# A list scheduler's table of durations is replaced, and the row copies at a block's end go to other tiles

## The chip, the cores and the metric

The kernel runs on one core of a Trainium2 chip. The metric is the device time of one execution in microseconds, as the median of several runs. A core has a matrix engine (PE), a vector engine (DVE), a scalar engine (ACT), a general engine (POOL), and a queue that only issues transfers (SP). Each works through its own list of instructions in a fixed order, and an instruction that waits holds back all that stand behind it on its engine.

## The reference

Attention over pooled keys and values, then two MLPs over 4608 tokens of width 512, all in float32:

```python
k_p, v_p = mean of k, v over groups of 8 positions     # 576 -> 72 per head
attn = softmax(q @ k_p.T / 8) @ v_p                    # 8 batches, 8 heads of 64
x = attn, heads side by side                           # 4608 x 512
h = x @ w_in                                           # 512 -> 2048
g = where(h >= 1, h, where(h <= -1, 0, (h + 1)**2 / 4))
y = g @ w_out                                          # 2048 -> 512
out = (sigmoid(y @ w_gate) * (y @ w_val)) @ w_out2     # 512 -> 1536 -> 512
```

## The kernel before, in words

A float32 product is made of three products of a cheaper format (`three`, L607 to L611): each operand is split into a high part, a cast, and a low part, the difference. The cast is made by ACT (L534), the difference by DVE (L543).

The tokens are cut into nine blocks of 512, the 2048 columns of `w_in` into sixteen steps of 128. Seven blocks go through the first MLP in the plain way described here, and the last two go through it later, by a scheme with seven products instead of eight, which is used for the second MLP too. In the first MLP step s (block s div 16, weight s mod 16) consists of two pieces of PE work:

- the **h step** s: four column products of three matmuls each, `h <- x, win` at L609 to L611, into one of two PSUM banks called h. The third matmul of a product, L611, is the first to read the low part of the weight `win`.
- the **y step** s: four products, `acc <- g, wj` at L609 to L611, which add to four accumulators called acc. For the first twelve steps it is four plain float32 products instead (L772, called plain products below, two matmul instructions each in the profile).

Between them ACT makes relu and square (L741, L743) and DVE the rest of g (L746), whose end also frees the h bank for h step s+2. ACT and DVE then split g, and split `wout_f` into `wj` (both L534 and L543).

While block 0 is worked on, the weights are fetched and prepared (`weight`, L556 to L600): abs and scaling on ACT (L580, L582), four bit operations on DVE (L585, L587, L590, L594), then cast and difference. Attention of later blocks goes on beside all of this, and after step 22 the weights of the second MLP are prepared and written to DRAM.

At the end of a block `out_rows` (L621) copies the four accumulators to SBUF, two to a tile, on ACT or DVE, and SP writes each tile to DRAM (`y`). For blocks 0 to 5 the first tile is `st`, with one buffer of its own, and the second is one of the two buffers of `raw`, which weight preparation also uses.

The order of instructions on each engine isn't written out. Each operation is entered by `op(engine, cost, key, fn, ...)` with a duration in microseconds. `Plan.issue` then plays a list scheduler: it keeps a modelled time for each engine, and of the operations that could start within 0.05 us of the earliest it issues the one with the smallest key. The durations decide nothing on the chip but this order, and which of two engines gets a copy that either could do. A result is taken to be usable 0.14 us after its duration ends. Transfers have their own model, which the change leaves alone.

Of the kernel before, what the change touches and what calls it, by code (L numbers as in the profile page):

```python
# [18 lines left out]
P = 128  # L19
POOL = 8  # L20
TB = 512
# [186 lines left out]
def pooled_attention_two_mlps(  # L208
# [77 lines left out]
    AC = {n: ac for n in ("kp", "q", "qT", "mx", "sm", "aq", "aT", "st")}  # L286
# [98 lines left out]
    def unit(j, p, T):  # L385
# [54 lines left out]
        for h in range(2):  # L440
# [106 lines left out]
    def reload(d, t, key, behind):  # L547
# [4 lines left out]
        op(ACT, 0.62, key - 2, lambda: nc.scalar.copy(out=t.t[:, 0], in_=vals()), r=[t], w=[t])  # L552
        op(DVE, 0.69, key - 1, lambda: nc.vector.tensor_tensor(
            out=t.t[:, 1], in0=vals(), in1=t.t[:, 0].bitcast(F32), op=ALU.subtract), r=[t], w=[t])

    def weight(w, m, cols, r, key, t=None, keep=None, spill=None):  # L556
# [37 lines left out]
        op(DVE, 0.7, key - 4, lambda: nc.vector.tensor_tensor(  # L594
# [18 lines left out]
    def columns(key, o, w, xs):  # L613
        last = []
        for c in range(KD):
# [3 lines left out]
            last = [op(PE, 0.65, key + 0.1 * c, mm, r=[w, xs[c]], w=[o], behind=last)]  # L619

    def out_rows(key, dst, accs, d=(), early=False):  # L621
        for i in range(2):
            st = buf_a("st", 1, [P, 2, TB]) if early and i == 0 else Buf(raw_p, "raw", 2, [P, 2, TB], fifo=None if early else True)
            for n, a in enumerate(accs[2 * i:2 * i + 2]):
                op((ACT, DVE), (0.48, 0.6), key, (
                    lambda st=st, a=a, n=n: nc.scalar.copy(out=st.t[:, n], in_=a.t),
                    lambda st=st, a=a, n=n: nc.vector.tensor_copy(out=st.t[:, n], in_=a.t)), r=[a], w=[st])
            op(SP, 0.475, key + 1, lambda st=st, i=i: nc.sync.dma_start(
                out=dst[2 * i * P:2 * (i + 1) * P, :].rearrange("(c p) t -> p c t", p=P), in_=st.t),
                r=[st], w=d, nbytes=P * DM * 8)  # L630


    zeros = memsets()
    xs_of = {}
# [65 lines left out]
    for j in range(NB1):  # L700
        if j >= XD:
            xs_of[j] = [buf_x() for _ in range(KD)]
            for c in range(KD):
                x, d = xs_of[j][c], x_d[j, c]
                T = due1(j * M1) - 12 + c
                op(SP, 0.475, T - 16, lambda x=x, d=d: nc.sync.dma_start(out=x.t[:, 1].bitcast(F32), in_=d.t), r=[d], w=[x], nbytes=P * TB * 4)
                high_part(T, x, Src(x, lambda t: t[:, 1].bitcast(F32)))
                op(DVE, 0.69, T + 1, lambda x=x: nc.vector.tensor_tensor(
                    out=x.t[:, 1], in0=x.t[:, 1].bitcast(F32), in1=x.t[:, 0].bitcast(F32), op=ALU.subtract), r=[x], w=[x])
        xs = xs_of.pop(j)  # L710
        for m in range(M1):
# [29 lines left out]
            op(ACT, 0.69, Tg, lambda t=t, hps=hps: nc.scalar.activation(  # L741
                out=t.t, in_=hps.t, func=AF.Relu, bias=half.t, scale=0.5), r=[hps, half], w=[t])
            op(ACT, 0.63, Tg + 1, lambda t=t: nc.scalar.activation(  # L743
                out=t.t, in_=t.t, func=AF.Square), r=[t], w=[t])
            o = g if plain else t
            op(DVE, 0.69, Tg + 2, lambda t=t, hps=hps, o=o: nc.vector.scalar_tensor_tensor(  # L746
# [22 lines left out]
            for c in range(KD):  # L769
# [143 lines left out]
    def out_part(gs, f, m, key, accs, last):  # L913
        g = buf_g()
        op2(ACT, 0.62, key - 5, lambda: nc.scalar.copy(out=g.t[:, 0], in_=gs.t[:, f]), r=[gs], w=[g])
        op2(DVE, 0.69, key - 4, lambda: nc.vector.tensor_tensor(
            out=g.t[:, 1], in0=gs.t[:, f], in1=g.t[:, 0].bitcast(F32), op=ALU.subtract), r=[gs, g], w=[g])
        w = w2[m]
        for c in range(4):
# [3 lines left out]
            last[c] = [op(PE, 0.65, key + 0.1 * c, mm, r=[w, g], w=[accs[c]], behind=last[c])]  # L923
# [10 lines left out]
    for i in range(MP):  # L934
# [4 lines left out]
        for n in range(2):  # L939
            sl, a21 = slots[n]  # L940
            for f in range(2):
                last = []
                for c in range(KD):
# [5 lines left out]
                    last = [op(PE, 0.65, T + 5.2 * n + 2.6 * f + 0.1 * c, mm, r=[sl, a21, xs[c]], w=[banks[n, f]], behind=last)]  # L949
# [3 lines left out]
        for f in range(2):  # L953
# [4 lines left out]
            op2(DVE, 0.69, T + 2.6 * f + 6, lambda t=t, f=f, gs=gs, pv=banks[1, f]: nc.vector.tensor_tensor(  # L958
# [45 lines left out]
    def out_pair(pr, hs, K0, KP):  # L1004
# [4 lines left out]
        def comb(key, h, n, x, y, alu, other=None):  # L1009
            op2(DVE, 0.69, key, lambda: nc.vector.tensor_tensor(out=h.t[:, n], in0=x(), in1=y(), op=alu),  # L1010
# [6 lines left out]
        def product(n, mat, o, start, what):  # L1017
            chain = []
            for i in range(MP):
# [14 lines left out]
                chain[:] = [op2(PE, 1.3, key, mm, r=[w, g] + ([] if start or i else o), w=o, behind=chain)]  # L1034
# [3 lines left out]
        def add(key, o, b, u):  # L1038
            for e in range(2):
                op2(DVE, 0.69, key, lambda e=e: nc.vector.tensor_tensor(  # L1040
# [47 lines left out]
        def to_bank(key, src, dst):  # L1088
            for e in range(2):
                op2(ACT, 0.6, key, lambda e=e: nc.scalar.copy(out=dst[e].t, in_=src.t[:, e]), r=[src], w=[dst[e]])  # L1090
# [300 lines left out]
```

## Time and profile before

| what | value |
|---|---|
| median of 3 runs | 1692.19 us (1691.58 to 1692.28) |
| the profiled execution | 1693.15 us |
| its span | 1691.4 us |
| PE busy | 1667.2 us, 99% |
| DVE, ACT, POOL busy | 69%, 57%, 14% |
| mean granted TensorE clock | 0.996 |

The span runs from the first to the last instruction of the program; what lies around it in the profiled execution is 1.75 us. Busy time of PE counts a matmul from its start to its modelled end, and matmuls overlap, so PE's idle time is what can be read from it, not its rate.

### The profile page before, as it was taken

How to read it: one execution, taken by the hardware profiler on the slowest of the kernel's cores; microseconds unless marked ns; L12 is line 12 of the kernel's file. 1: busy time of each engine (PE TensorE's matmuls, PEld its weight loads, DVE VectorE, ACT ScalarE, POOL GpSimd, SP SyncE). 2: the span in 40 equal slices, each digit the busy share in tenths (PEclk: the TensorE clock that was granted, in tenths of full speed). 3: DMA queues.
4: the chain of work that ended last, by engine and by line, in shares of the span. 5: the costliest groups of instructions: out<-in, count | busy, mean ns of one | idle time of the engine just before them, and what ended most of it. 6: DMA issues, size and time to landing. Idle time of an engine off the chain costs nothing.

```text
span 1691.4 us, 26119 instructions
## 1 busy us (share of the span) xinstructions
PE 1667.2 (99%) x8484; PEld 1323.8 (78%) x8484; DVE 1168.6 (69%) x2166; ACT 967.8 (57%) x2140; POOL 238.3 (14%) x338
## 2 busy tenths in 40 slices
PE   7999999999999999999999999999999999999998
PEld 5657777777777777788888888878888888888886
DVE  7988767878787878846778856574448445744476
ACT  6767556676676668643466735454435454544344
POOL 1224323333433222100000002100000000000000
PEclk8999999999999999999999999999999999999999
DMA  8889867777877656547887879997889788977774
GB/s 218 246 250 244 203 138 203 230 217 195 233 201 191 175 162 211 175 159 303 326 275 239 292 237 370 360 343 215 234 257 304 211 238 274 280 194 205 206 219 135
DMA packets 308647, 396.07 MB, mean 234 GB/s; under 512 B 133664, under 2 KB 173856, under 8 KB 306976
## 3 DMA queue, kind: packets, MB, share of 16 engines
q1 hardware_dynamic: 270848, 285.97, 57.1%
q0 software_dynamic: 37664, 108.44, 20.6%
q8 instruction: 68, 1.11, 0.3%
q14 instruction: 67, 0.55, 0.1%
HBM read 272.11 MB, written 112.72 MB: 228 GB/s over the span
## 4 chain that ended last, share of the span: by engine, by line
PE 89%; DMA 5%; DVE 3%; SPq 1%; ACT 1%; issue 1%; POOL 0%; DVEq 0%; POOLq 0%; ACTq 0%
PE acc L609 12%; PE h L609 12%; PE acc L611 12%; PE acc L610 12%; PE h L610 11%; PE h L611 11%; PE a L609 5%; PE a L611 5%; PE a L610 5%; PE a L508 2%; DMA kv<-in_k_dram 2%; PE a L436 1%; PE acc L772 1%; DMA raw<-in_moe_w_out_dram 1%; SPq L487 1%
## 5 line engine op out<-in xcount | busy, mean ns | idle before, releaser
L834 DVE TENSOR_TENSOR g<-win,g 128x512 fp32r<-128x512 f32 x168 | 114.8, 689 | 113.1 <-ACT g L833 111.7
L609 PE MATMUL h<-x,win 128*128 128x512 f32 x448 | 183.4, 409 | 2.1 <-DVE t L746 2.1
L611 PE MATMUL h<-x,win 128*128 128x512 f32 x448 | 175.1, 391 | 1.3 <-DVE win L543 1.3
L610 PE MATMUL h<-x,win 128*128 128x512 f32 x448 | 175.3, 391 | 0.4 <-DVE x L522 0.4
L833 ACT CAST g<-win 128x512 fp32r<-128x512 f32 x168 | 104.3, 624 | 111.8 <-PE acc L611 90.5
L609 PE MATMUL acc<-g,wj 128*128 128x512 f32 x400 | 161.3, 403 | 0.0
L610 PE MATMUL acc<-g,wj 128*128 128x512 f32 x400 | 156.5, 391 | 0.0
L611 PE MATMUL acc<-g,wj 128*128 128x512 f32 x400 | 156.2, 391 | 0.0
L609 PE MATMUL acc<-g,wo 128*128 128x512 f32 x360 | 140.1, 389 | 0.7 <-ACT g L833 0.7
L611 PE MATMUL acc<-g,wo 128*128 128x512 f32 x360 | 140.1, 389 | 0.0
L610 PE MATMUL acc<-g,wo 128*128 128x512 f32 x360 | 140.1, 389 | 0.0
L609 PE MATMUL h<-x,ws 128*128 128x512 f32 x336 | 131.3, 391 | 0.4 <-ACT h L1335 0.4
L610 PE MATMUL h<-x,ws 128*128 128x512 f32 x336 | 131.0, 390 | 0.2 <-DVE x L829 0.2
L611 PE MATMUL h<-x,ws 128*128 128x512 f32 x336 | 130.8, 389 | 0.0
L741 ACT ACTIVATE t<-h,half 128x512 f32<-128x512 f32 x112 | 77.2, 689 | 89.0 <-PE h L611 88.0
L609 PEld LDWEIGHTS h<-x,win 128*128 128x128 f32 x448 | 84.1, 188 | 28.4 <-issue 6.0
L611 PEld LDWEIGHTS h<-x,win 128*128 128x128 f32 x448 | 84.1, 188 | 20.7 <-DVE win L543 2.6
L610 PEld LDWEIGHTS h<-x,win 128*128 128x128 f32 x448 | 84.2, 188 | 19.2 <-issue 2.4
L609 PEld LDWEIGHTS acc<-g,wj 128*128 128x128 f32 x400 | 75.1, 188 | 24.3 <-issue 7.4
L611 PEld LDWEIGHTS acc<-g,wj 128*128 128x128 f32 x400 | 75.1, 188 | 16.8 <-DVE wj L543 0.3
L534 ACT CAST wj<-wout_f 128x512 fp32r<-128x512 f32 x100 | 61.8, 620 | 43.4 <-PE acc L611 37.1
L610 PEld LDWEIGHTS acc<-g,wj 128*128 128x128 f32 x400 | 75.1, 188 | 14.6 <-DVE f L590 0.2
(308 smaller groups left out, 4062.0 us busy)
## 6 DMA issues: line engine op xcount, KB each, us to landing
ws<-seven SPq DMA_DIRECT2D x412, 256.0 KB
wo<-seven_o SPq DMA_DIRECT2D x144, 256.0 KB
seven<-f POOLq DMA_DIRECT2D x64, 256.0 KB, 3.8
seven<-wa POOLq DMA_DIRECT2D x8, 1792.0 KB, 7.7
seven_o<-wo POOLq DMA_DIRECT2D x42, 256.0 KB, 5.8
w<-f POOLq DMA_DIRECT2D x36, 256.0 KB, 4.2
wo<-seven SPq DMA_DIRECT2D x36, 256.0 KB
win<-in_moe_w_in_dram SPq DMA_DIRECT2D x16, 512.0 KB
```

The lines of the kernel that those rows point to most:

```text
L436: nc.tensor.matmul(out=scs[h].t[r0 % P:r0 % P + D, r0 // P * C:r0 // P * C + C], lhsT=qT.t[D * h:D * h + D, r0:r0 + D], rhs=kts[b % 2, p]. ...
L487: op(SP, 0.65, T + 10, lambda a=a, bl=bl, n=n: nc.sync.dma_start(out=aT.t[32 * bl:32 * bl + n, a].rearrange("c h t j -> c (h t j)"), in_=a ...
L508: nc.tensor.matmul(out=px.t[D * h:D * h + D, lo:hi], lhsT=vps[b % 2, p].t[:, h], rhs=rhs, start=True, stop=True)
L534: ACT: (0.52, lambda: nc.scalar.copy(out=dst.t[:, 0], in_=src())),
L609: nc.tensor.matmul(out=o, lhsT=wh, rhs=xh, start=start, stop=False, skip_group_check=more)
L610: nc.tensor.matmul(out=o, lhsT=wh, rhs=xl, start=False, stop=False, skip_group_check=more)
L611: nc.tensor.matmul(out=o, lhsT=wl, rhs=xh, start=False, stop=stop, skip_group_check=more)
L741: op(ACT, 0.69, Tg, lambda t=t, hps=hps: nc.scalar.activation(out=t.t, in_=hps.t, func=AF.Relu, bias=half.t, scale=0.5), r=[hps, half], w=[t])
L772: nc.tensor.matmul(out=accs[c].t, lhsT=wj.t[:, c * P:(c + 1) * P], rhs=g.t, start=m == 0, stop=m == M1 - 1)
L833: op2(ACT, cost, key, lambda: nc.scalar.copy(out=out_hi(), in_=val()), r=[src, b], w=[b])
L834: op2(DVE, cost, key + 0.5, lambda: nc.vector.tensor_tensor(out=out_lo(), in0=val(), in1=out_hi().bitcast(F32), op=ALU.subtract), r=[src, ...
```

## The change

Some thirty numbers in calls of `op` are replaced. Those for 128x512 operations of DVE that were 0.69 become 0.61; those of ACT that were 0.6 to 0.69 become 0.485 to 0.585 at most places, and one pair of alternatives 0.6 and 0.61; a group of three matmuls goes from 0.65 to 0.68, a pair of such groups from 1.3 to 1.36, a plain product from 0.9 to 1.03; the exponentials of all blocks but the first go from 0.52 to 0.3.

Apart from the numbers, `out_rows` for blocks 0 to 4 takes both of its tiles from the eight buffers of `x`, and for block 5 both from `raw`; the tile `st` is gone. The loads of x for blocks 4, 5 and 6 are ordered behind the row copies of the block two before.

```diff
-    AC = {n: ac for n in ("kp", "q", "qT", "mx", "sm", "aq", "aT", "st")}
+    AC = {n: ac for n in ("kp", "q", "qT", "mx", "sm", "aq", "aT")}
...
-                op(ACT, 0.3 if first else 0.52, T + 5, lambda t=t, h=h, view=view, mx=mx: nc.scalar.activation(
+                op(ACT, 0.3, T + 5, lambda t=t, h=h, view=view, mx=mx: nc.scalar.activation(
...
-            last = [op(PE, 0.65, key + 0.1 * c, mm, r=[w, xs[c]], w=[o], behind=last)]
+            last = [op(PE, 0.68, key + 0.1 * c, mm, r=[w, xs[c]], w=[o], behind=last)]
...
     def out_rows(key, dst, accs, d=(), early=False):
+        rows = []
         for i in range(2):
-            st = buf_a("st", 1, [P, 2, TB]) if early and i == 0 else Buf(raw_p, "raw", 2, [P, 2, TB], fifo=None if early else True)
+            st = Buf(x_p, "x", 2 * KD, [P, 2, TB], fifo=None) if early > 0 else Buf(raw_p, "raw", 2, [P, 2, TB], fifo=None if early else True)
...
-                op(SP, 0.475, T - 16, lambda x=x, d=d: nc.sync.dma_start(out=x.t[:, 1].bitcast(F32), in_=d.t), r=[d], w=[x], nbytes=P * TB * 4)
+                op(SP, 0.475, T - 16, lambda x=x, d=d: nc.sync.dma_start(out=x.t[:, 1].bitcast(F32), in_=d.t), r=[d], w=[x], behind=rows_of[j - 2], nbytes=P * TB * 4)
...
-            op(DVE, 0.69, Tg + 2, lambda t=t, hps=hps, o=o: nc.vector.scalar_tensor_tensor(
+            op(DVE, 0.61, Tg + 2, lambda t=t, hps=hps, o=o: nc.vector.scalar_tensor_tensor(
...
-                last_y[c] = [op(PE, 0.9 if plain else 0.65, due1(s + 2) + 2.6 + 0.1 * c, mm, r=[wj, g], w=[accs[c]], behind=last_y[c])]
+                last_y[c] = [op(PE, 1.03 if plain else 0.68, due1(s + 2) + 2.6 + 0.1 * c, mm, r=[wj, g], w=[accs[c]], behind=last_y[c])]
...
-        out_rows(due1(s + 2) - 10, y_d[j].t, accs, [y_d[j]], j < NB1 - 1)
+        rows_of[j] = out_rows(due1(s + 2) - 10, y_d[j].t, accs, [y_d[j]], 1 if j + 2 < NB1 else -1 if j < NB1 - 1 else 0)
```

The table moves instructions on every engine. Both programs have the same matmuls on PE. Three places follow, as the built programs list them.

PE around h step 15, the last to use a fresh weight. In the rows of before the y step 13 (`acc_936`, the last of its four accumulators) stands ahead of h step 15 (`h_1925`):

```order
L611 MATMUL acc_927<-g_1819,wj_1780 128x512
L609 MATMUL acc_936<-g_1819,wj_1780 128x512
L610 MATMUL acc_936<-g_1819,wj_1780 128x512
L611 MATMUL acc_936<-g_1819,wj_1780 128x512
L609 MATMUL h_1925<-x_694,win_1894 128x512
L610 MATMUL h_1925<-x_694,win_1894 128x512
L611 MATMUL h_1925<-x_694,win_1894 128x512
```

The same place of the changed program, where `h_1910` is h step 15 and `g_1828`, `wj_1743` are those of y step 13:

```order
L609 MATMUL h_1910<-x_827,win_1843 128x512
L610 MATMUL h_1910<-x_827,win_1843 128x512
L611 MATMUL h_1910<-x_827,win_1843 128x512
L609 MATMUL acc_915<-g_1828,wj_1743 128x512
L610 MATMUL acc_915<-g_1828,wj_1743 128x512
L611 MATMUL acc_915<-g_1828,wj_1743 128x512
```

The twelve matmuls of y step 13 moved from ahead of h step 15 to behind it. In the same way the four plain products of y step 10 moved from ahead of h step 12 to behind it.

PE at h steps 36 and 37 in block 2. Of before, the end of h step 36 (`h_3311`), the first product of h step 37 (`h_3338`) and the beginning of y step 34 (`acc_3202`):

```order
L610 MATMUL h_3311<-x_2785,win_1085 128x512
L611 MATMUL h_3311<-x_2785,win_1085 128x512
L609 MATMUL h_3338<-x_2200,win_1159 128x512
L610 MATMUL h_3338<-x_2200,win_1159 128x512
L611 MATMUL h_3338<-x_2200,win_1159 128x512
L609 MATMUL acc_3202<-g_3315,wj_3297 128x512
L610 MATMUL acc_3202<-g_3315,wj_3297 128x512
```

Of the change, where `h_3363` is h step 36 and `acc_3269` belongs to y step 34:

```order
L610 MATMUL h_3363<-x_2801,win_1054 128x512
L611 MATMUL h_3363<-x_2801,win_1054 128x512
L609 MATMUL acc_3269<-g_3302,wj_3309 128x512
L610 MATMUL acc_3269<-g_3302,wj_3309 128x512
L611 MATMUL acc_3269<-g_3302,wj_3309 128x512
```

The y step now stands between the two h steps. From step 17 on, an h step begins right behind another h step at eleven places of before (h steps 37 and 59 among them) and at one of the change (h step 99).

ACT at the end of block 1. In the rows of before the accumulator copies into `st` and `raw` stand apart:

```order
L626 COPY st<-acc 128x512 x2
L743 ACTIVATE t<-t 128x512
L682 CAST f<-raw 128x256
L534 CAST wj<-wout_f_136 128x512
L534 CAST g<-t 128x512
L582 ACTIVATE raw<-raw 128x512
L682 CAST f<-raw 128x256
L448 ACTIVATE e_sb,sm<-a,mx 128x72
L580 ACTIVATE f<-raw 128x512
L741 ACTIVATE t<-h,half 128x512
L448 ACTIVATE e_sb,sm<-a,mx 128x72 x4
L626 COPY raw<-acc 128x512
```

In the rows of the change (its line numbers are two higher from here on) they go to `x`:

```order
L627 COPY x<-acc 128x512
L745 ACTIVATE t<-t 128x512
L684 CAST f<-raw 128x256
L627 COPY x<-acc 128x512
L684 CAST f<-raw 128x256
L627 COPY x<-acc 128x512
```

The three copies that ACT makes moved together, ahead of the casts and exponentials that stood between them.

## Rows read from the trace of the kernel before

**Rows 1.** The profile's page: the span, and what PE was busy.
```profile
span 1691.4 us, 26119 instructions
PE 1667.2 (99%) x8484; PEld 1323.8 (78%) x8484; DVE 1168.6 (69%) x2166; ACT 967.8 (57%) x2140; POOL 238.3 (14%) x338
```

**Rows 2.** Windows in us: length, then busy time and count by engine, clock, DMA.
```profile
0.00:42.00 42.00, 31.87 (x268) 22.69 (x268) 31.37 (x73) 28.05 (x99) 5.36 (x11) 0.84 0.87 218
42.00:155.00 113.00, 110.15 (x617) 70.02 (x616) 99.11 (x203) 78.70 (x199) 31.07 (x35) 1.00 0.89 245
155.00:700.00 545.00, 542.94 (x3287) 423.19 (x3287) 432.97 (x910) 366.52 (x984) 172.17 (x236) 1.00 0.72 197
700.00:1120.00 420.00, 416.56 (x1823) 340.74 (x1823) 285.86 (x489) 232.88 (x409) 29.67 (x56) 1.00 0.81 286
1120.00:1655.00 535.00, 534.95 (x2361) 442.60 (x2360) 299.48 (x465) 248.97 (x429) 0.00 (x0) 1.00 0.81 238
```

**Rows 3.** Waits of PE: who waited for whom, us in total, times, longest.
```profile
PE h L609 <- DVE t L746: 2.1, 2, 1.8
PE h L611 <- DVE win L543: 1.3, 2, 1.1
PE a L354 <- DMA kv<-in_k_dram: 1.0, 1, 1.0
PE a L609 <- ACT a L1335: 0.9, 2, 0.7
PE a L360 <- DVE kp L339: 0.5, 1, 0.5
PE h L610 <- DVE x L522: 0.4, 1, 0.4
PE h L609 <- ACT h L1335: 0.4, 1, 0.4
```

**Rows 4.** Timeline of DVE near 38 us: start and duration in us.
```profile
37.53 0.68 DVE L590 SCALAR_TENSOR_TENSOR f<-raw,f 128x512 uint32<-128x512 uint32 x1
38.14 0.68 DVE L522 SCALAR_TENSOR_TENSOR x<-acc,x 128x512 fp32r<-128x512 f32 x1
38.74 0.67 DVE L543 TENSOR_TENSOR win<-f,win 128x512 fp32r<-128x512 f32 x1
```

**Rows 5.** The chain of waits, one piece: start, us, eight matmuls of four plain products.
```profile
92.69 3.43 PE acc L772 x8
```

**Rows 6.** Timeline near 102 us: ACT held by PE, then DVE held by ACT.
```profile
101.50 0.69 ACT L741 ACTIVATE t<-h,half 128x512 f32<-128x512 f32 x1 [1.94 <-PE h L611]
...
102.73 0.69 DVE L543 TENSOR_TENSOR win<-f,win 128x512 fp32r<-128x512 f32 x1 [2.42 <-ACT win L534]
```

**Rows 7.** Waits of ACT and of DVE in the window 30 to 155 us.
```profile
ACT t L741 <- PE h L611: 13.2, 11, 2.3
...
DVE win L543 <- ACT win L534: 4.7, 3, 2.4
```

**Rows 8.** Timeline: weights' low parts and the matmuls reading them, h steps 12, 15.
```profile
120.61 0.69 DVE L543 TENSOR_TENSOR win<-f,win 128x512 fp32r<-128x512 f32 x1 [0.45 <-ACT win L534]
...
122.22 0.39 PE L611 MATMUL h<-x,win 128*128 128x512 f32 x1
...
142.79 0.67 DVE L543 TENSOR_TENSOR win<-f,win 128x512 fp32r<-128x512 f32 x1
...
143.52 0.49 PE L611 MATMUL h<-x,win 128*128 128x512 f32 x1 [1.05 <-DVE win L543]
```

**Rows 9.** Timeline at h step 37: PE's wait, and DVE's work on wj 34.
```profile
272.73 0.50 PE L609 MATMUL h<-x,win 128*128 128x512 f32 x1 [0.28 <-DVE t L746]
...
272.60 0.68 DVE L543 TENSOR_TENSOR wj<-wout_f,wj 128x512 fp32r<-128x512 f32 x1
```

**Rows 10.** Timeline at h step 59: ACT held by a transfer, DVE, PE's wait.
```profile
406.44 0.67 ACT L582 ACTIVATE raw<-raw 128x512 int32<-128x512 uint32 x1 [4.91 <-DMA raw<-in_moe_w_out_dram]
...
410.73 0.67 DVE L543 TENSOR_TENSOR wj<-wout_f,wj 128x512 fp32r<-128x512 f32 x1
...
410.86 0.50 PE L609 MATMUL h<-x,win 128*128 128x512 f32 x1 [1.78 <-DVE t L746]
```

More of the change, by code (lines that the diff above doesn't have):

```diff
@@ L551, in reload @@
            r=[d], w=[t], behind=behind, nbytes=P * DM * 4)
-        op(ACT, 0.62, key - 2, lambda: nc.scalar.copy(out=t.t[:, 0], in_=vals()), r=[t], w=[t])
-        op(DVE, 0.69, key - 1, lambda: nc.vector.tensor_tensor(
+        op(ACT, 0.52, key - 2, lambda: nc.scalar.copy(out=t.t[:, 0], in_=vals()), r=[t], w=[t])
+        op(DVE, 0.61, key - 1, lambda: nc.vector.tensor_tensor(
             out=t.t[:, 1], in0=vals(), in1=t.t[:, 0].bitcast(F32), op=ALU.subtract), r=[t], w=[t])
@@ L593, in weight @@
         val = keep or f
-        op(DVE, 0.7, key - 4, lambda: nc.vector.tensor_tensor(
+        op(DVE, 0.6, key - 4, lambda: nc.vector.tensor_tensor(
             out=val.t.bitcast(I32), in0=f.t.bitcast(I32), in1=low().bitcast(I32), op=ALU.add),
@@ L630, in out_rows @@
                 r=[st], w=d, nbytes=P * DM * 8)
+        return rows
     zeros = memsets()
-    xs_of = {}
+    xs_of, rows_of = {}, {}
     for p in range(NPAIR):
@@ L914, in out_part @@
         g = buf_g()
-        op2(ACT, 0.62, key - 5, lambda: nc.scalar.copy(out=g.t[:, 0], in_=gs.t[:, f]), r=[gs], w=[g])
-        op2(DVE, 0.69, key - 4, lambda: nc.vector.tensor_tensor(
+        op2(ACT, 0.52, key - 5, lambda: nc.scalar.copy(out=g.t[:, 0], in_=gs.t[:, f]), r=[gs], w=[g])
+        op2(DVE, 0.61, key - 4, lambda: nc.vector.tensor_tensor(
             out=g.t[:, 1], in0=gs.t[:, f], in1=g.t[:, 0].bitcast(F32), op=ALU.subtract), r=[gs, g], w=[g])
@@ L922, in mm @@
                       w.t[:, 0], w.t[:, 1], m == 0, m == M2 - 1)
-            last[c] = [op(PE, 0.65, key + 0.1 * c, mm, r=[w, g], w=[accs[c]], behind=last[c])]
+            last[c] = [op(PE, 0.68, key + 0.1 * c, mm, r=[w, g], w=[accs[c]], behind=last[c])]
     lasts = [[] for _ in range(4)]
@@ L948, in mm @@
                         three(o.t, a[0], a[1], xs[c].t[:, 0], xs[c].t[:, 1], c == 0, c == KD - 1)
-                    last = [op(PE, 0.65, T + 5.2 * n + 2.6 * f + 0.1 * c, mm, r=[sl, a21, xs[c]], w=[banks[n, f]], behind=last)]
+                    last = [op(PE, 0.68, T + 5.2 * n + 2.6 * f + 0.1 * c, mm, r=[sl, a21, xs[c]], w=[banks[n, f]], behind=last)]
         if i == MARK0:
@@ L1033, in mm @@
                               start and i == 0, i == MP - 1, not start)
-                chain[:] = [op2(PE, 1.3, key, mm, r=[w, g] + ([] if start or i else o), w=o, behind=chain)]
+                chain[:] = [op2(PE, 1.36, key, mm, r=[w, g] + ([] if start or i else o), w=o, behind=chain)]
                 if (n, i) == MARK:
@@ L1039, in add @@
             for e in range(2):
-                op2(DVE, 0.69, key, lambda e=e: nc.vector.tensor_tensor(
+                op2(DVE, 0.61, key, lambda e=e: nc.vector.tensor_tensor(
                     out=o.t[:, e], in0=b[e].t, in1=u.t[:, e], op=ALU.add), r=[b[e], u], w=[o])
@@ L1089, in to_bank @@
             for e in range(2):
-                op2(ACT, 0.6, key, lambda e=e: nc.scalar.copy(out=dst[e].t, in_=src.t[:, e]), r=[src], w=[dst[e]])
+                op2(ACT, 0.485, key, lambda e=e: nc.scalar.copy(out=dst[e].t, in_=src.t[:, e]), r=[src], w=[dst[e]])
         def to_sbuf(key, src, dst):
             for e in range(2):
-                op2(ACT, 0.6, key, lambda e=e: nc.scalar.copy(out=dst.t[:, e], in_=src[e].t), r=[src[e]], w=[dst])
+                op2(ACT, 0.485, key, lambda e=e: nc.scalar.copy(out=dst.t[:, e], in_=src[e].t), r=[src[e]], w=[dst])
         def sums(at, f):
@@ L1217, in minus @@
             u = late("u", 3, [P, TB])
-            op2(DVE, 0.69, key, lambda: nc.vector.tensor_tensor(
+            op2(DVE, 0.61, key, lambda: nc.vector.tensor_tensor(
                 out=u.t, in0=x().bitcast(F32), in1=y().bitcast(F32), op=ALU.subtract), r=reads, w=[u])
@@ L1284, in mm @@
                                   start and k == 0, k == 1, not start)
-                    op(PE, 1.3, T + H * pos, mm, r=[w] + xx + ([] if start else [o]), w=[o])
+                    op(PE, 1.36, T + H * pos, mm, r=[w] + xx + ([] if start else [o]), w=[o])
                 def add(key, o, b, u):
-                    op2(DVE, 0.69, key, lambda: nc.vector.tensor_tensor(out=o.t, in0=b.t, in1=u.t, op=ALU.add),
+                    op2(DVE, 0.61, key, lambda: nc.vector.tensor_tensor(out=o.t, in0=b.t, in1=u.t, op=ALU.add),
                         r=[b, u], w=[o])
@@ L1298, in finish @@
                         if u:
-                            op2(DVE, 0.69, key, lambda: nc.vector.tensor_tensor(
+                            op2(DVE, 0.61, key, lambda: nc.vector.tensor_tensor(
                                 out=g.t[:, bb], in0=b.t, in1=u.t, op=ALU.add), r=[b, u], w=[g])
@@ L1328, in keep @@
                     if kind == "in":
-                        op2((ACT, DVE), (0.6, 0.69), key, (lambda: nc.scalar.copy(out=u.t, in_=b.t),
+                        op2((ACT, DVE), (0.485, 0.61), key, (lambda: nc.scalar.copy(out=u.t, in_=b.t),
                                                            lambda: nc.vector.tensor_copy(out=u.t, in_=b.t)), r=[b], w=[u])
                     else:
-                        op2(ACT, 0.6, key, lambda: nc.scalar.copy(out=u.t, in_=b.t), r=[b], w=[u])
+                        op2(ACT, 0.485, key, lambda: nc.scalar.copy(out=u.t, in_=b.t), r=[b], w=[u])
                 def to_bank(key, src, dst):
```

26 lines of the change are left out of this document (13 added, 13 removed).

## The prediction

> **What bounds the kernel now.** I began with the page: PE is busy in 99% of the span, DVE in 69%, ACT in 57% [rows 1]. Since PE's matmuls overlap, a busy PE says nothing of its rate; the windows by stage do. From 1120 to 1655 us PE runs 2361 matmuls in 535 us and is idle for 0.05, so one takes 535/2361 = 0.2266 us and a group of three 0.680 [rows 2]. The number of matmuls does not change. So a new order can win only what PE idles: length minus PE's busy time is 10.1 us up to 42 us, then 2.85 (to 155), 2.06 (to 700), 3.44 (to 1120) and 0.05 [rows 2]. The first is nearly all the first loads, before which there is nothing to reorder. About 8.4 us remain, half a per cent of the time. PE's waits say who owns them: 2.1 us for the rest of g (L746), 1.3 for the low part of a weight, 1.0 for a transfer of k and v, 0.5 for kp, 0.4 for x, and 0.9 and 0.4 for copies at L1335 [rows 3]. PE reads these in order, so the question at each wait is what the new order puts there, and the timelines around the waits answer it.
>
> **The new durations, against the trace.** A 128x512 operation of DVE lasts 0.68 us, but the next one starts after 0.60 or 0.61 [rows 4]; so the new 0.61 is the time for which it holds the engine. Its result comes at 0.68, and the plan still allows 0.61 + 0.14 = 0.75 for that; the old number allowed 0.83. So the new plan starts successors 0.08 earlier and is not too early for the end of the operation by itself. The 0.68 for three matmuls is what PE takes (above). The 1.03 for a plain product is not: eight instructions of four products took 3.43 us, 0.857 each [rows 5], so the number moved from 0.04 too long to 0.17 too long. Twelve y steps have four each, all before 155 us; there the plan has PE later than it is.
>
> [...]
>
> **Up to 42 us.** One copy at L474 goes from ACT to DVE, so DVE has 0.6 us more ahead of the last x (L522). PE already waits 0.4 there [rows 3]. By itself that costs 0.6; but PE is stopped later in this phase by weights that transfers bring, and the two do not add. Taken: 0.
>
> **42 to 155 us, fresh weights.** Because the plan now believes plain products long, it sends h steps ahead of them: h step 12 comes ahead of the four plain products of y step 10, so 3.43 us earlier [rows 5], and h step 15 ahead of twelve matmuls of y step 13, 12 x 0.2266 = 2.72 earlier [rows 2]. If the weights came when they come now, PE would wait. The low part that h step 12 needs ended at 120.61 + 0.69 = 121.30 and was read at 122.22 [rows 8]: slack 0.92, wait 3.43 - 0.92 = 2.5. At h step 15 there is none, PE already waits 1.05 [rows 8]: wait 2.72 more. The second contains the first, since 2.5 us lost at h step 12 makes the later steps that much later. Against this, 0.5 for kp is then covered [rows 3]: +2.2. The DVE order also puts about 2.3 us of other work ahead of the low part of weight 13: +4.5 if none is hidden. The other bound is that all waits of this stage go: -2.85.
>
> What decides is whether weights come earlier too. In this stretch ACT waited 13.2 us, in 11 places, for the end of an h step, and in its queue the cast of the next weight stands behind that wait; DVE waited 4.7 us for that cast [rows 7]. One instance: ACT's relu is held 1.94 by PE, and then DVE's low part 2.42 by ACT [rows 6]. An earlier h step releases ACT earlier, the cast earlier and the low part earlier. If half of DVE's 4.7 comes back, weights are 2.35 earlier where 2.72 is needed: +0.4, against the 0.5 for kp. Taken: 0.
>
> **155 to 700 us.** Both waits here are alike: 0.28 at h step 37, 1.78 at h step 59 [rows 9, 10]. An h step stood right behind another, and the second needs the bank that L746 frees. The change puts a y step there, which needs no bank. That removes 2.06. What is late next is the y step's own operand: its third matmul, 0.45 after its start, needs the low part of wj. At h step 37 PE became free at 272.73 - 0.28 = 272.45, so it is wanted at 272.90, and it ended at 272.60 + 0.68 = 273.28: 0.38 [rows 9]. At h step 59 it is wanted at 410.86 - 1.78 + 0.45 = 409.53 and ended at 410.73 + 0.67 = 411.40: 1.87 [rows 10]. With DVE as late as now, 2.25 replace 2.06: +0.2. DVE was late at step 59 since ACT stood 4.91 us behind a transfer into `raw` [rows 10]; the row copies of blocks 0 to 4 no longer take part in that ring, so such a stop may be shorter, but the loads of these weights still share it. New places could arise too: DVE's order carries 3 to 8 us of attention and later weights ahead of critical operations over long stretches, and can, being idle 545 - 433 = 112 us here [rows 2]. Bounds -2.06 and +1; taken: half gained, -1.0.
>
> **Row copies in x tiles.** PE waits for no such copy now: among its waits none is for L626 [rows 3]. The copy into x waits until the block's h step 15 has read that tile; a y step and more lies behind that, so it is free. For blocks 4 to 6 the loads of x now stand in SP's queue behind the copies of the block two before, and behind them the loads of k, v and w. Those copies end a whole block earlier, 16 steps of eight groups, 16 x 8 x 0.68 = 87 us, and the stores ahead of them in the queue wait for the same copies already. Taken: 0. Without that cover a late x would stop PE for a transfer, a cast and a difference, by the nearest rows up to 4.91 + 0.69 + 0.69 = 6.3 us a block [rows 6, 10].
>
> **From 700 us.** PE's order hardly changes. Waits behind copies at L1335 are 0.9 and 0.4 [rows 3]; ACT and DVE get these copies in a slightly different order. If they go, -1.3; if they double, +1.3; taken -0.4. The last thirty instructions of ACT, DVE and SP are in the same order, so the end stays.
>
> **Sum.** 0 + 0 - 1.0 + 0 - 0.4 = -1.4. The profiled execution took 1693.15, the span 1691.4 [rows 1] and 1.75 around it; it becomes 1691.75. It lay 0.96 above the median of the runs, so the median becomes 1690.8.
>
> **Rivals.** *Slower: h steps come before their weights.* If ACT's wait for PE does not turn into earlier weights, the first stage costs +2.2 to +4.5, say +3, and the y steps at 37 and 59 wait for wj, +0.2 to +1, with nothing back later: +4, 1696.2. It decides from about 4 us of PE waiting for L543. For it: DVE's larger share of other work, and h step 15 with no slack [rows 8]. Against: the 13.2 us of ACT [rows 7]. *The waits only move*, each replaced by one as long behind it: 1692.2. For it: 2.25 against 2.06 above. *All inner waits go*: -2.85 - 2.06 - 1.3 = -6.2, 1686.0. For it: DVE has 112 us of slack and a y step is now between nearly all h steps; against: at h step 59 a transfer and not the order was late [rows 10]. [...]
>
> **Chances.** Forecast 0.43, waits only move 0.22, all go 0.20, slower 0.13, DVE held 0.02. A measurement here can tell about 0.2%, 3.4 us. Faster by more than that, below 1688.8: nearly all of "all go" and a fifth of the forecast, since its terms are each uncertain by 1 to 3 us: 0.29. Slower, above 1695.6: most of the slower rival and little of the fourth: 0.12. The rest, 0.59. The range for 8 in 10 runs from 1686.0, where all waits go, to 1695.5, where the slower rival is about half paid over the forecast.
>
> **What would show it.** In PE's waits after: L746 is gone or under 0.5, and no wait of more than 0.5 for wj takes its place; PE waits for win at L543 under 2 us in all; ACT's 13.2 and DVE's 4.7 between 30 and 155 us [rows 7] are smaller. If they are as large and PE's waits for win are 4 us or more, the step on fresh weights is wrong. If PE waits for x at a block's start or for a copy at a block's end, the step on the x tiles is wrong. If the window from 1120 to 1655 keeps 0.05 us idle, nothing has touched the stage that has no wait. A difference above 6.2 us in either direction would need a cause that is none of these.

## The result, and the profile after

The changed kernel takes 1717.5 us (median of 5 runs, 1708.52 to 1718.25) against 1692.19 (5 runs, 1689.79 to 1694.17), 25 us more by the medians. The ratio of the means is 1.0136, 95% interval 1.0108 to 1.0164; every ratio below is one of means too. The profiled execution took 1718.01. The forecast was 1690.8 and its range ended at 1695.5.

The page of the changed kernel, its span and PE's busy time:

```profile
span 1716.2 us, 26114 instructions
PE 1676.4 (98%) x8484; PEld 1328.0 (77%) x8484; DVE 1163.2 (68%) x2162; ACT 976.5 (57%) x2144; POOL 237.9 (14%) x338
```

The span is 24.8 us longer than in [rows 1], PE is busy for 9.2 more with the same 8484 matmuls. The same windows as in [rows 2] (length, then busy time and count of PE, PEld, DVE, ACT, POOL, clock, DMA):

```profile
0.00:42.00 42.00, 30.95 (x268) 21.64 (x268) 31.78 (x74) 27.53 (x98) 5.62 (x11) 0.92 0.86 219
42.00:155.00 113.00, 108.92 (x608) 68.47 (x607) 98.66 (x204) 76.28 (x192) 35.34 (x40) 1.00 0.88 242
155.00:700.00 545.00, 533.67 (x3215) 415.83 (x3214) 420.19 (x891) 365.18 (x975) 165.23 (x228) 0.99 0.70 193
700.00:1120.00 420.00, 414.26 (x1809) 337.32 (x1809) 276.94 (x477) 229.85 (x404) 31.56 (x60) 1.00 0.77 270
1120.00:1655.00 535.00, 533.04 (x2347) 439.80 (x2346) 293.09 (x454) 249.58 (x432) 0.17 (x1) 1.00 0.81 245
```

Between 155 and 700 us PE idles 545 - 533.67 = 11.3 us where it idled 2.06, and it gets through 72 matmuls fewer. As the clock times of the two programs drift apart, the fair comparison is by position: take PE's matmuls in the order in which they start, cut where the windows of before cut them (after 268, 884, 4170 and 5992), and measure how long PE needs for each piece. The pieces take 41.9, 113.2, 545.1, 420.0 and 566.3 us before, and 42.0, 115.2, 561.8, 425.6 and 566.9 after. So 16.7 of the 25 us are lost between matmuls 885 and 4170 (the first MLP from block 1 on, with the attention of later blocks beside it) and 5.5 between 4171 and 5992 (the passage to the second MLP). I call these two the **MLP piece** and the **passage**.

What PE waited for between 155 and 700 us in the changed kernel (who for whom, us in total, times, longest):

```profile
PE a L508 <- ACT e_sb L448: 5.6, 4, 2.5
PE a L436 <- DVE kt L367: 4.4, 3, 2.2
PE a L508 <- DMA aT<-aq: 1.2, 3, 0.5
```

The waits for L746 of [rows 3] are gone. In their place PE waits in the attention of later blocks: its second product (`values`, L508) for exponentials that still read the PSUM bank it needs, and its first (`scores`, L436) for the pooled keys. PE waited for none of these between 155 and 700 us in before. One of them, seen from ACT and then from PE in the timeline (start, duration, operation, in brackets the wait before it):

```profile
530.23 0.63 ACT L745 ACTIVATE t<-t 128x512 f32<-128x512 f32 x1
533.91 0.65 ACT L582 ACTIVATE raw<-raw 128x512 int32<-128x512 uint32 x1 [3.04 <-DMA raw<-in_moe_w_gate_dram]
534.46 0.30 ACT L448 ACTIVATE e_sb<-a,mx 128x72 f32<-128x72 f32 x1
...
535.35 0.62 ACT L534 CAST g<-t 128x512 fp32r<-128x512 f32 x1
535.86 0.33 ACT L448 ACTIVATE e_sb<-a,mx 128x72 f32<-128x72 f32 x1
```

```profile
533.41 0.39 PE L611 MATMUL h<-x,win 128*128 128x512 f32 x1
536.33 1.08 PE L508 MATMUL a<-aT,vp 72*64 72x384 f32 x8 [2.53 <-ACT e_sb L448]
```

ACT stands 3.04 us behind the transfer of a weight of the second MLP, which the first does not need. Behind it in ACT's queue stand the exponentials, and behind those PE, for 2.53. At 467 us it is alike, with 4.64 behind such a transfer and 2.47 on PE, but there eight other operations, three of them copies of the accumulators, stand between the transfer and the exponentials. ACT was held as long in before, 4.91 [rows 10], and cost PE 1.78.

And the wait is not all. Windows around the wait at 467 us, in the same columns as above:

```profile
460.00:467.40 7.40, 7.40 (x62) 5.64 (x60) 2.63 (x6) 3.20 (x7) 0.62 (x2) 1.00 0.67 229
467.40:470.00 2.60, 0.20 (x1) 0.00 (x0) 2.60 (x7) 2.60 (x12) 1.29 (x2) 0.96 0.83 216
470.00:476.40 6.40, 6.34 (x26) 4.68 (x27) 5.85 (x12) 4.03 (x14) 3.73 (x5) 0.50 0.99 355
476.40:484.00 7.60, 7.60 (x34) 6.29 (x33) 5.74 (x12) 5.77 (x10) 0.81 (x2) 0.99 0.83 214
```

Behind PE's idle 2.6 us the granted clock is 0.50 of full speed, and comes back. The same stands behind the waits at 160 us and at 534. The three stretches, cut where the clock falls and rises:

```profile
162.60:166.00 3.40, 3.40 (x33) 2.68 (x26) 3.19 (x7) 2.25 (x5) 1.30 (x2) 0.50 0.96 294
469.80:476.60 6.80, 6.54 (x27) 4.87 (x28) 6.16 (x12) 4.23 (x15) 3.92 (x5) 0.50 0.99 351
538.00:541.50 3.50, 3.50 (x10) 2.73 (x9) 3.04 (x8) 0.47 (x1) 0.61 (x1) 0.51 0.50 122
```

In all three, matmuls of 512 columns in a row start 0.427 us apart (the median), where 0.2266 is what one takes at 1.00 [rows 2]. Half of 3.4 + 6.8 + 3.5, my estimate from the clock, is 6.8 us of lost work. With 11.3 - 2.06 = 9.3 of longer waits that makes 16.1 of the 16.7 us of this piece.

### The profile page after: what moved, and what is told of

Read it like the earlier page. It is cut to its first block, busy times and chain, and to the rows that moved or that the text cites. A ratio compares the mean times of both kernels' runs of the same rounds, so it can differ in the third digit from the quotient of the medians.

```text
span 1716.2 us, 26114 instructions
## 1 busy us (share of the span) xinstructions
PE 1676.4 (98%) x8484; PEld 1328.0 (77%) x8484; DVE 1163.2 (68%) x2162; ACT 976.5 (57%) x2144; POOL 237.9 (14%) x338
## 4 chain that ended last, share of the span: by engine, by line
PE 72%; DMA 14%; DVE 5%; ACT 3%; issue 2%; SPq 2%; POOL 0%; DVEq 0%; POOLq 0%; ACTq 0%
PE acc L609 10%; PE acc L611 10%; PE acc L610 10%; PE h L609 10%; PE h L610 9%; PE h L611 9%; PE a L609 4%; PE a L611 4%; PE a L610 4%; DMA raw<-in_moe_w_out_dram 2%; DMA kv<-in_k_dram 1%; PE a L508 1%; DMA seven<-f 1%; SPq L487 1%; DMA q<-in_q_dram 1%
## 5 line engine op out<-in xcount | busy, mean ns | idle before, releaser
L610 PE MATMUL acc<-g,wj 128*128 128x512 f32 x400 | 157.1, 393 | 0.0
L748 DVE SCALAR_TENSOR_TENSOR t<-t,h 128x512 f32<-128x512 f32 x100 | 68.0, 680 | 45.0 <-ACT t L745 44.3
L609 PEld LDWEIGHTS acc<-g,wj 128*128 128x128 f32 x400 | 75.7, 189 | 22.7 <-issue 5.6
L534 ACT CAST g<-t 128x512 fp32r<-128x512 f32 x100 | 62.2, 622 | 52.1 <-DVE t L748 51.0
L611 PEld LDWEIGHTS acc<-g,wj 128*128 128x128 f32 x400 | 75.7, 189 | 16.5
```

What stands on the lines that cost most here:

```text
L534: ACT: (0.52, lambda: nc.scalar.copy(out=dst.t[:, 0], in_=src())),
L609: nc.tensor.matmul(out=o, lhsT=wh, rhs=xh, start=start, stop=False, skip_group_check=more)
L610: nc.tensor.matmul(out=o, lhsT=wh, rhs=xl, start=False, stop=False, skip_group_check=more)
L611: nc.tensor.matmul(out=o, lhsT=wl, rhs=xh, start=False, stop=stop, skip_group_check=more)
L748: op(DVE, 0.61, Tg + 2, lambda t=t, hps=hps, o=o: nc.vector.scalar_tensor_tensor(out=o.t, in0=t.t, scalar=1.0, in1=hps.t, op0=ALU.min, op1 ...
```

## The experiments

Two words are used below. The **distance** is the number of matmuls of 512 columns between `scores` and the next `values` in PE's built order; its middle value is 24 before and 12 in the change. The **margin** is what lies between the planned end of an operation and the time at which the plan lets its user start. The plan's 0.14 us is one part of it, a duration that is too long another.

**Which part.** Four kernels. In the first and the second only this line differs, from the change and from before:

```diff
# e1_exp_back, from the change
-                op(ACT, 0.3, T + 5, lambda t=t, h=h, view=view, mx=mx: nc.scalar.activation(
+                op(ACT, 0.3 if first else 0.52, T + 5, lambda t=t, h=h, view=view, mx=mx: nc.scalar.activation(
# e2_exp_alone, from before: the same line the other way round
```

The third is before with the new `out_rows`, its calls and the order of the x loads; the fourth is the change without them.

```diff
# e3_x_alone, from before (e4_x_back: the change without it)
-            st = buf_a("st", 1, [P, 2, TB]) if early and i == 0 else Buf(raw_p, "raw", 2, [P, 2, TB], fifo=None if early else True)
+            st = Buf(x_p, "x", 2 * KD, [P, 2, TB], fifo=None) if early > 0 else Buf(raw_p, "raw", 2, [P, 2, TB], fifo=None if early else True)
```

> The change, with the exponentials of all blocks but the first back at 0.52. First theory (the short price of the exponentials sends PE's second attention product, `values`, too soon behind the first, `scores`): in PE's order the middle distance between the two is 12 matmuls of 512 columns in the change, 24 before and 18 here, so most of the 8.4 us that PE waits for exponentials and most of the lost clock go: 1696 to 1702. Second theory (the other durations together make the plan too tight, the exponentials are only where it shows): 1712 or more. Third theory (the x tiles): 1712 or more, as they stay.

Measured 1710.51, 1.0112 of before (1.0092 to 1.0132). PE's waits for exponentials fell from 8.4 us to 0.8, but others came (4.3 for weights, 2.2 for kp, 2.1 for the bank that L748 frees), and the MLP piece took 554.7. Some 7 of the 25 us came back, not most of them, and the time lies between the ranges of the theories.

> The kernel before, with only the price of these exponentials at 0.3. The middle distance from scores to values is 15 matmuls. First theory: PE waits for exponentials for several us and loses clock, 1703 to 1715. Second and third theory: 1690 to 1695, as before.

Measured 1700.74, 1.0053 (1.0039 to 1.0067), between the two expectations. Slower, but not where expected. The MLP piece took 544.0, less than before, and matmuls 269 to 884 took 109.7 (113.2). The loss is the passage, 433.5 against 420.0. PE's longest wait there, 2.5 of 12.9 us, is for a weight, and DVE waits for its load:

```profile
772.61 0.43 DVE L879 TENSOR_TENSOR raw<-f,wb 128x256 f32<-128x256 f32 x1 [7.36 <-DMA wb<-w]
```

```profile
776.96 0.50 PE L611 MATMUL a<-x,wb 128*128 128x512 f32 x1 [2.54 <-DVE wb L829]
```

The load is late since SP issues it late: SP stands 12.2 us at the load into a tile that a store still reads. The waits of SP's queue between 740 and 800 us have it:

```profile
SPq L865 <- DMA seven<-wb: 24.9, 2, 12.7
```

That a long stand of SP must cost time is not shown: in before it stands 25.5 us at the same line, from 711 us on, and the passage takes 420.0.

> The kernel before, with only the row copies in x tiles and the order of the x loads, all durations old. The middle distance is 21. First and second theory: 1689 to 1696. Third theory (copies in x free the ring of raw, so that preparation runs ahead into late transfers and ACT stands still with exponentials behind it): 1703 or more.

Measured 1704.5, 1.0076 (1.0062 to 1.009). The x tiles alone cost 12 us in the median. In the profiled execution the MLP piece lost 2.0 and the passage 8.6, with SP held 12.2 and 12.7 us at the same loads as in the run above. The third theory named this time, but not the place. ACT's waits for transfers into `raw` between 155 and 700 us did grow, from 21.5 us to 31.0, yet little came of it in the MLP piece, and the passage has no exponentials.

> The change, with the row copies back in st and raw. The middle distance is 12 as in the change. First and second theory: 1710 to 1720, as the change. Third theory: 1700 or less.

Measured 1717.7, 1.0148 (1.0126 to 1.017): as the change. So the x tiles cost 12 us among the old numbers and nothing in all among the new. Neither of these parts is the cause by itself: what an edit costs depends on the order that the others make.

**One engine's numbers at a time, and the size of the step.** All four start from before.

```diff
# e5_dve_alone: 17 lines such as this one, and the 0.7 of L594 to 0.6
-            op(DVE, 0.69, Tg + 2, lambda t=t, hps=hps, o=o: nc.vector.scalar_tensor_tensor(
+            op(DVE, 0.61, Tg + 2, lambda t=t, hps=hps, o=o: nc.vector.scalar_tensor_tensor(
# e6_pe_alone: 0.65, 1.3 and 0.9 to 0.68, 1.36 and 1.03
# e7_act_alone: ACT's numbers, without the exponentials
# e8_dve_longer: 0.69 to 0.70; e12_dve_half: 0.69 to 0.65 (L594 stays at 0.7 in both)
```

> The kernel before, with only DVE's numbers new (0.61). First theory (shorter numbers leave less work between a result and the matmul that needs it, and PE waits for what was covered): slower in the first MLP, 1696 to 1706, with new waits of PE there. Second theory (any other order loses, since the one of before happens to fit the late transfers of the stage between the two MLPs): no loss up to 700 us, 5 to 13 us lost from there to 1120: 1697 to 1705. Third theory (0.61 is right and by itself harmless): 1690 to 1694.

Measured 1705.4, 1.009 (1.007 to 1.0111). The MLP piece took 558.4, 13.3 more than before, and half of that is one wait:

```profile
PE acc L609 <- ACT raw L626: 6.5, 1, 6.5
```

At a block's end PE needs the accumulators, whose copy into `raw` stands in ACT's queue behind eleven operations, most of them for later weights; one of them waits for a store:

```profile
680.20 0.41 ACT L682 CAST f<-raw 128x256 fp32r<-128x256 f32 x1 [0.68 <-DMA seven<-f]
681.15 1.07 ACT L626 COPY raw<-acc 128x512 f32<-128x512 f32 x2 [0.55 <-DVE f L683]
```

> The kernel before, with only PE's numbers new (0.68, 1.36, 1.03). The middle distance from scores to values is 20 matmuls, 24 before. First theory: fewer matmuls are thought enough as cover, so slower in the first MLP, 1696 to 1704. Second theory: 5 to 13 us lost between 700 and 1120 alone, 1697 to 1705. Third theory: 1690 to 1694.

Measured 1706.78, 1.0099 (1.0082 to 1.0116), above all three ranges. The profiled execution, the fastest of the four at 1704.09, lost 5.7 us in the passage, 2.1 in matmuls 269 to 884, 2.1 behind matmul 5992 and 0.8 in the MLP piece.

> The kernel before, with only ACT's numbers new, those of the exponentials old. First theory: 1694 to 1702, by waits of PE for casts and g. Second theory: 5 to 13 us lost between 700 and 1120 alone, 1697 to 1705. Third theory: 1690 to 1694.

Measured 1704.04, 1.0077 (1.0054 to 1.01): 9.0 us lost in the MLP piece, 4.1 in the passage. The time is above the first theory's range and in the second's, but most of the loss is where the first puts it.

> The kernel before, with DVE's 0.69 made 0.70 at all places: nothing is believed shorter, only the order is another one. First theory: 1689 to 1695, as before, or faster. Second theory (any other order loses): 1697 or more, with the loss between 700 and 1120 us. Third theory: 1690 to 1695.

Measured 1694.07, 1.0018 (1.0009 to 1.0028), in the first theory's range and in the third's. This new order, from a number 0.01 longer, costs about 3 us (1.5 to 4.7 by the interval).

> The kernel before, with DVE's 0.69 made 0.65, half of the way to 0.61. First and fourth theory (what is lost grows with the cover that is taken away, +14 us at 0.61): 1695 to 1702. Second theory (the loss depends on the order alone and not on the size of the step): as 0.70, 1692 to 1697, or as 0.61, without a trend.

Measured 1696.91, 1.003 (1.0019 to 1.0042), which lies in both ranges, so that the time does not decide. With DVE's number at 0.70, 0.69, 0.65 and 0.61 the ratio is 1.0018, 1, 1.003 and 1.009, and the MLP piece takes 547.3, 545.1, 550.0 and 558.4 us. Over these values the loss grows with the step. But each value is one order, the last rests in good part on the one wait of 6.5 us, and the last run below shows 12 us lost by an order alone: that the size of the step matters is suggested here, not shown.

**What the too long numbers paid for: late transfers, or time at each step?** Two kernels plan all transfers to land 2 us later, five change the 0.14.

```diff
# e9_late_transfers, from the change; e11_late_transfers_before, from before
-                free[eng], o.end = max(t, lanes[-8] + lat), lanes[-1]
+                free[eng], o.end = max(t, lanes[-8] + lat), lanes[-1] + 2.0
# e10, e15, e17, from the change: 0.4, 0.6, 0.3; e16, e18, from the change without x tiles: 0.4, 0.5
-LATENCY = 0.14
+LATENCY = 0.4
```

> The change, with every transfer planned to land 2 us later. Of the transfers that POOL issues, those of 256 KB land 3.8 to 6.0 us after issue and those of 512 KB 4.6 to 6.2, the plan believes 2.3 and 3.0 where none is ahead of them. Fourth theory (the too long durations of before paid for transfers that come later than planned; with true durations ACT and DVE reach instructions that wait for a transfer too early, and what PE needs stands behind them): most of the 25 us comes back, 1693 to 1705. First theory in its narrow form (only the short exponentials and DVE numbers count, whatever they covered): 1710 to 1720, as the change.

Measured 1712.28, 1.0119 (1.0091 to 1.0148); the MLP piece took 558.2. The time is the first theory's and not the fourth's. PE's waits for exponentials are gone from the MLP piece, but one at a block's end has taken their place:

```profile
PE acc L609 <- ACT raw L627: 7.7, 1, 7.7
```

(The landing times in the expectation are medians by group; two groups of 256 KB lie outside, at 3.3 and 7.8 us in before.)

> The kernel before, with every transfer planned to land 2 us later. Fourth theory: the waits for late transfers that are left in it (1.78 of PE at h step 59 behind a transfer into raw) go, 1685 to 1692. Second theory (any other order loses): 1694 or more, with the loss between 700 and 1120 us.

Measured 1713.09, 1.0134 (1.0113 to 1.0156), as the second theory had it: the passage took 433.0, 12.9 more than before. Waits for the bank that L746 frees are still there (2.3 us). This later landing time brings neither table of numbers near its forecast.

> The change, with a result taken to be usable 0.40 us after its duration instead of 0.14. If what is missing is time between a result and its next user, at each step of a chain (first theory, narrow form), this gives it back: 1696 to 1706. If it is transfers (fourth theory), little: 1708 to 1718.

Measured 1702.29, 1.0068 (1.0049 to 1.0088): 15 of 25 us are back.

> The change, with a result usable 0.60 us after its duration instead of 0.14 (at 0.40 15 us of 25 came back). Margin theory: the 3286 matmuls up to 700 us take no longer than in before (545 us), in all 1695 to 1703. If 0.40 was a lucky order: 1705 to 1718.

Measured 1715.77, 1.0143 (1.0129 to 1.0157): both numbers of the margin theory are missed, and the whole lies in the range of the lucky order. In all nothing is gained, yet the MLP piece took 551.4 (expected 545), 10 less than in the change. Of that 7.7 us are spent ahead of it: the first 884 matmuls took 164.8 against 157.1.

> The change with 0.40 for the usable result, and the row copies back in st and raw. If the x tiles cost their 12 us with any durations: 1690 to 1696. If that loss belongs to the order that they gave among the old numbers: 1699 to 1708.

Measured 1697.11, 1.0041 (1.0023 to 1.006), between the two expectations. What PE waited for from 160 to 700 us, in the change without x tiles (the four largest) and then with 0.40 besides (all):

```profile
PE a L508 <- ACT e_sb L448: 5.7, 4, 3.4
PE a L508 <- DMA kv<-in_v_dram: 2.4, 1, 2.4
PE a L436 <- DVE kt L367: 1.9, 2, 1.6
PE acc L609 <- ACT raw L626: 1.0, 3, 0.7
```

```profile
PE a L508 <- DVE wj L543: 0.6, 1, 0.6
```

> The change, with a result usable 0.30 us after its duration. With 0.40 and 0.60 the 3286 matmuls of PE from the 885th on took 548.8 and 551.4 us, with 0.14 561.8. Margin theory: a dose between gives a time between, 549 to 558 us for that stretch. If any order gives a time by chance: outside of it. The whole: 1700 to 1715.

Measured 1700.91, 1.006 (1.0043 to 1.0077); the MLP piece took 548.4. That is just under the margin theory's range and so, by the letter, outside of it: a gain that goes with the dose is not shown, since 0.30 gives as much as 0.40 and more than 0.60. What this run adds is a third dose that has the gain.

> The change with 0.50 for the usable result, and the row copies back in st and raw (0.40 gave 543.3 us for the same stretch, 0.14 gave 563.4). Margin theory: 543 to 548 us for that stretch. Chance: 552 or more. The whole: 1694 to 1708, the stages before and behind that stretch being better or worse by their own orders.

Measured 1703.58, 1.0073 (1.0056 to 1.0089); the MLP piece took 547.8, in the range.

How long PE needed, by position, in the kernels with all new durations (my count from the traces, us). The first two pieces are taken together here, since with more margin 15 to 22 matmuls of 512 columns move from the first into the second:

```
margin  x tiles     1-884   885-4170   4171-5992
0.14    new         157.1      561.8       425.6   the change
0.14    old         161.3      563.4       420.7   e4
0.30    new         160.9      548.4       421.6   e17
0.40    new         160.5      548.8       421.0   e10
0.40    old         157.6      543.3       423.8   e16
0.50    old         166.0      547.8       421.9   e18
0.60    new         164.8      551.4       424.0   e15
(old numbers, 0.14) 155.2      545.1       420.0   before
```

All five with more margin get back 10 to 20 us of the MLP piece. Up to there four of them lose 3 to 8 us against the kernel with 0.14 and the same tiles, and one (0.40, old tiles) gains 3.7; with 0.40 and 0.50 PE waits there for the high part of `win` (2.6 to 3.1 us). The kernels with the new numbers and 0.14 (the change, e4, e9, and e1 with the old exponentials) took 554.7 to 563.4 in the MLP piece, above all five. It isn't the distance: that is 12 with 0.30, as in the change, and the waits for exponentials are gone from the MLP piece all the same. Nor is it just that with more margin ACT comes later to its transfers. Its waits for those into `raw` between 155 and 700 us (sums of the rows of that view) are 39.5 us in the change, 31.4 with 0.30 and 9.6 in e9, and the MLP piece takes 561.8, 548.4 and 558.2.

**The short exponentials where they seemed to gain.**

```diff
# e13_exp_to_block3, from before (e14_exp_to_block1: j < 2)
-                op(ACT, 0.3 if first else 0.52, T + 5, lambda t=t, h=h, view=view, mx=mx: nc.scalar.activation(
+                op(ACT, 0.3 if j < 4 else 0.52, T + 5, lambda t=t, h=h, view=view, mx=mx: nc.scalar.activation(
```

> The kernel before, with the exponentials at 0.3 for blocks 1 to 3 only. With 0.3 for all blocks PE's first 884 matmuls ended 4.1 us sooner, the next 3286 took 1.0 less, and the 1822 between the two MLPs 13.4 more, where SP stood 12.2 us at a load of w for a buffer. Queue theory (the loss between the MLPs is that one order of SP): the gain stays, the loss goes, 1685 to 1690. Margin theory (0.3 takes cover away wherever it stands): 1692 to 1700.

Measured 1693.06, 1.0009 (0.9998 to 1.002): no difference, which is in the margin theory's range and not in the queue theory's. The passage is back to 420.1 and matmuls 269 to 884 keep their gain (109.7). Both agree with the queue theory's mechanism, but 1.4 us went in the MLP piece, and the 2.5 us that the profiled execution is shorter do not show in the medians.

> The kernel before, with the exponentials at 0.3 for block 1 only, those that run while the weights are fetched. Queue theory: 1686 to 1690. Margin theory: 1691 to 1696.

Measured 1701.83, 1.0062 (1.0049 to 1.0074). Neither theory. The piece of the fresh weights gains about the same, 3.8 us, and then the MLP piece loses 12.3, though its numbers are those of before and only block 1's differ. A change of order early in the program moves everything behind it, also where nothing was edited; here that costs as much as any of the edits.

## Why the prediction was wrong

**What bounds the kernel.** PE, as forecast, and nothing speaks against the 8.4 us to be won: none of the kernels here is faster than before. That bounds the gain, not the loss. I took each wait of before and asked what becomes of it, and put next to no price on what does not wait now. The signs that I had named looked at the same places: L746 gone, no wait for wj, little for `win`, 13.2 and 4.7 smaller all came true, and the kernel is 25 us slower.

**Up to 42 us.** 42.0 against 41.9, but by luck. PE was stopped by no weight in this window of before: its waits there are 7.3 us for q, 2.3 for kt and 0.4 for x. The 0.6 us that I took for hidden stand there as a wait, and PE idles 42 - 30.95 = 11.05 us against 10.1:

```profile
PE acc L470 <- DVE x L522: 0.7, 1, 0.7
```

What made up for it is the granted clock, 0.92 in this window against 0.84 [rows 2], which I had not priced.

**42 to 155 us, fresh weights.** The mechanism was right, its sizes were not. Waits of ACT and of DVE between 30 and 155 us, the first two to be held against [rows 7]:

```profile
ACT t L743 <- PE h L611: 1.8, 2, 1.2
DVE win L543 <- ACT win L534: 1.4, 2, 0.7
ACT win L534 <- DVE f L594: 14.9, 10, 3.1
```

13.2 and 4.7 us became 1.8 and 1.4, and PE waits 0.3 us for `win` in all. But ACT is not free in exchange: its wait for the last bit operation of a weight grew from 2.5 to 14.9. Most weights came earlier (the low part for h step 15 ended at 141.2 instead of 143.5), the one for h step 12 did not (122.0 instead of 121.3), and h step 12 read it only 0.2 us earlier than in before and not 3.43. The rival of h steps ahead of their weights is refuted. But 4.0 us of attention waits came here (2.8 for exponentials, 1.2 for aT) that I had put at nothing; the piece lost 1.9.

**155 to 700 us: the step that failed.** I wrote "bounds -2.06 and +1". The 2.06 did go, as forecast, and the wj of the y step was not late. The upper bound was wrong: measured +16.7. Two terms were put at nothing without a reason: PE's waits in the attention of later blocks, 0.5 us here in before, and the clock that a wait of PE costs. That new places of waiting could arise I had seen, and I capped them at +1, because DVE's 112 idle microseconds looked like room for the 3 to 8 us more of other work that it carries ahead of critical operations. Idle time over a stretch is no cover at a place. The runs show what is there in place of the bound. PE waits 9.3 us more, all of its waits stand in front of attention products, and the clock lost behind three long waits adds 6.8 by the estimate above. As to why, more margin at each result gives 10 to 20 us of this piece back in all five kernels that have it. The reading of that is that shorter numbers let the plan put a matmul close behind the result it needs, so that when ACT or DVE is held, by a transfer in the timelines above, PE is held too; the timelines show two such places, and that it is so at every step is argued.

**DVE held 0.69.** No run shows this term of the chances, which I gave 0.02: behind a 128x512 operation of DVE the next one starts after 0.60 or 0.61 us in before [rows 4], and in the changed kernel three that last 0.68 each start at 37.58, 38.18 and 38.78 us and the next operation at 39.38, 0.60 apart.

**Row copies in x tiles.** Taken 0; in the change that holds (1717.7 without them). Among the old numbers they cost 12 us, in the passage, which I had not looked at for them.

**From 700 us: the second step that failed.** "PE's order hardly changes" is no bound on time: +5.5 where I allowed 1.3. In the change 3.8 of it is longer waiting of PE, 2.2 in one wait for g (L918). Which wait takes it differs from kernel to kernel. In e2 and e3 SP's order of loads stands 12 us at a tile, and where that order was absent (e13) their loss was too; but the change, e1 and e11 lost 5.5, 7.8 and 12.9 without it. A common cause is not shown.

**What stays open.** Why the x tiles cost nothing in the change; which single step of the attention lacks the margin; what costs the time in the passage; and why e14 loses 12 us in blocks that it does not edit. I do not know either whether some table of numbers beats before: of the 18 orders tried besides the change one was level with it and none faster.

## What to carry to other kernels

In a list schedule whose bound engine is 99% busy, a duration is also a margin: replacing a too long one by the measured one takes cover away at every step. Margin put back by name returned most of one stage here and cost time in another, and no kernel with the new numbers came back to the time of before. A forecast from waits that exist tells what can be won; what can be lost has to be read from the places where an engine stands behind a transfer, and from what the bound engine needs of it next. And an edit of such a table can't be priced part by part: here five parts that cost 8 to 16 us each when alone, some 63 in all, made 25 together.

## What the hardware showed that was not expected

A wait of PE can cost about as much again in clock: 6.8 us, by the estimate above, behind three waits of 7.2 together. After the waits of 2.2 to 2.5 us at 160, 467 and 534 us the granted clock was 0.50 for 3.4, 6.8 and 3.5 us. It was not the length of the wait alone: the wait of 2.22 us at 855 us, with plain 128x512 matmuls on both sides and no attention product, left it at 1.00:

```profile
855.00:857.10 2.10, 0.05 (x1) 0.00 (x0) 2.10 (x4) 1.01 (x2) 0.00 (x0) 1.00 0.98 375
857.20:861.00 3.80, 3.73 (x16) 3.10 (x17) 3.63 (x7) 2.21 (x5) 0.00 (x0) 1.00 0.98 377
```

Nor do the attention products beside the wait decide it. In `e2_exp_alone` two waits lie among plain 128x512 matmuls: the one of 2.54 us at 774 us left the clock at 1.00, the one of 2.22 at 851 was followed by 0.50.

```profile
774.00:777.00 3.00, 0.46 (x3) 0.04 (x1) 3.00 (x8) 2.70 (x3) 0.00 (x0) 1.00 0.22 75
776.60:779.60 3.00, 2.64 (x11) 2.17 (x12) 3.00 (x5) 1.57 (x3) 0.06 (x1) 1.00 0.00 0
780.00:790.00 10.00, 10.00 (x46) 8.29 (x45) 6.65 (x12) 3.39 (x5) 1.14 (x3) 1.00 0.98 412
...
851.50:853.70 2.20, 0.00 (x0) 0.00 (x0) 1.43 (x3) 1.92 (x3) 0.00 (x0) 1.00 0.50 154
854.20:857.60 3.40, 3.40 (x9) 2.66 (x9) 3.21 (x7) 2.40 (x4) 0.00 (x0) 0.50 0.11 22
```

And in `e17_latency_03` a wait of 2.58 us right in front of an attention product, at 406 us, left it at 1.00:

```profile
405.60:408.10 2.50, 0.05 (x1) 0.00 (x0) 1.21 (x2) 1.82 (x7) 0.00 (x0) 1.00 0.99 291
408.20:412.00 3.80, 3.77 (x28) 3.09 (x29) 1.57 (x5) 2.63 (x7) 1.49 (x2) 1.00 0.84 166
```

What decides it stays open. The five runs of the change fit a price in clock: three at a mean clock of 0.993 or 0.994 took 1717.5 to 1718.3 us, two at 0.998 took 1708.5 and 1712.5. The runs of before beside them lay within 4.4 us of each other.
